# Half-size fetch, cast and transpose of one batch's tokens, earlier scores, and one shared transpose at the end: a change to a fused attention and feed-forward kernel

## The chip, the cores and the metric

The kernel runs on one core of a Trainium2 chip. The metric is the device time of one execution, in microseconds (us). Three timed runs of the kernel before gave 217.05, 218.31 and 218.33 us, median 218.31. A fourth, profiled execution took 216.83 us; all lines of the profile come from that one. Its span, from the first to the last instruction that the profiler recorded, is 214.6 us.

The engines: PE multiplies matrices (PEld is its loading of stationary weights), ACT (ScalarE) does activations and copies, DVE (VectorE) reductions, 32x32 transposes and elementwise work, POOL (GpSimd) copies and issues DMAs, SP (SyncE) only issues DMAs. Each engine runs its own instructions strictly in order.

## The reference

```
scores = scale * x @ state^T            # per batch and head: 512 tokens x 32 states, D = 64
a      = softmax over the 32 states;    xread = a @ state
a2     = softmax over the 512 tokens of scores^T;   sread = a2 @ x
rows   = concat(xread, sread) per batch, all 8 heads side by side (512 wide)
out    = leaky_relu(rows @ w_in) @ w_out          # 512 -> 2048 -> 512
```

There are 8 batches of 8 heads. The output has 8 x (512 + 32) rows of 512 fp32 numbers.

## The kernel before, in words

**Stages of one batch.** The tokens x of a batch (1 MB fp32) are fetched (`load_x`, L97), cast to bf16 in `xb` (`cast_x`, L104) and transposed to `xT`, from batch 2 on by a DMA that transposes (`a_xt_dma`, L188). `a_scores` (L201) multiplies `xT` with the batch's states into the PSUM tile `sc`, of which there is one. The states of batches 2 and 3 come through `load_state(0)` (L165, eight DMAs), a cast on POOL and a transposing DMA into `st_t` (`state_t`, L174). From `sc` two softmaxes start. Over the states: `a_shift` on DVE (maximum L215, its spreading L223, subtraction L225), `a_exp` on ACT (L232), `a_probs` on DVE (L237 to L247), which gives `aT`. Over the tokens: `a_max2` on DVE (L265), two `a_exp2` on ACT (L273), `a_probs2` on DVE (L286), then a transposing DMA (`a_a2t`, L291; batches 0 and 1 share one, L298) and `a_sread` (L305: 16 matmuls, two small ACT copies into `sr_t`).

**The feed-forward part.** `a_m` (L324) multiplies states with `w_in`, a quarter of its columns at a time, and `m_evict` (L344) copies the result to `M`. `ff1` (L354) then makes one of 16 slices of the hidden layer: two matmuls of `M` with `aT` into a PSUM tile `ph` (there are two), and a leaky ReLU on ACT (L362). `piece` (L379) does four of the 16 accumulating matmuls of one 128-row output tile `py` (L385); after the fourth piece the tile is copied by ACT or DVE (L394) and stored by SP (L400).

**Order.** It is written out by hand, engine by engine: each engine's instructions stand in the order of the calls. The main loop goes over batches b and, in each, over 16 steps s. A step is one `ff1` of b and, in batches 2 to 7 in every step, in batch 1 in every odd step, one `piece`. Everything else is hung on a step: in batch 1 (L673 to L698) the scores of batch 2 at step 4, its exponentials at steps 7, 9 and 11; in batch b from 2 on the scores of b+1 at step 1, the shared steps 5 to 7 for the exponentials, `a_sread` of b at step 8, and the transposes for it at step 0.

**Around the change.** Ahead of batch 1's loop (L638 to L667) stands batch 1's attention, mixed with batch 0's output pieces, and the preparation of batch 2: its `load_x` was issued long before on POOL's DMA queue, behind all weights (L539). At L648 comes the last eviction of batch 1's `M` on ACT, then its two `a_exp2` on ACT (L650), `state_t(0)` (L652), the cast of batch 2's heads 0 to 3 on ACT (L653) and 4 to 7 on POOL (L654), the transposing DMA of all of `xb` (L656), `a_probs(1)` on DVE, pieces of batch 0, and the stores with `load_x(3)` between them (L662 to L665).

Of the kernel before, what the change touches and what calls it, by code (L numbers as in the profile page):

```python
# [27 lines left out]
def kernel(  # L28
# [66 lines left out]
    xs, xl = {}, {}  # L95

    def load_x(b, eng):  # L97
        xl[b] = xpool.tile([P, H, NT * D], FP32, name="xl", tag="xl", bufs=2)
        eng.dma_start(xl[b][:], x[b].rearrange("h (p t) d -> p h (t d)", t=NT))

    def open_xb(b):
        xs[b] = xpool.tile([P, NT, H, D], BF16, name="xb", tag="xb")

    def cast_x(b, h0, h1, copy):  # L104
        copy(  # L105
            xs[b][:, :, h0:h1].rearrange("p t h d -> p h t d"),
            xl[b][:, h0:h1].rearrange("p h (t d) -> p h t d", t=NT),
        )

    def cast_x0(h0, h1, copy):  # L110
        u = h0 // NK
        copy(
            xs[0][:, :, h0:h1].rearrange("p t h d -> p h t d"),
            xf[u][:, h0 - NK * u:h1 - NK * u].rearrange("p h (t d) -> p h t d", t=NT),
        )

# [48 lines left out]
    def load_state(i):  # L165
        lo, hi = groups[i]
        for k in range(NK):
            for g in range(2):
# [2 lines left out]
                    state[lo:hi, 2 * k + g].rearrange("b n d -> n b d"),  # L171
                )

    def state_t(i):  # L174
        POO(stb[i][:], stf[i][:])
        nc.sync.dma_start_transpose(st_t[i][:], stb[i][:].rearrange("p b q -> p (b q)"))


# [4 lines left out]
    def a_open(a, b):  # L183
        a.b = b
        a.xb = xs[b]
        a.xT = att.tile([P, NT, NK, P], BF16, name="xT", tag="xT")

    def a_xt_dma(a):  # L188
        nc.sync.dma_start_transpose(
            a.xT[:].rearrange("p t k q -> p (t k) q"),  # L190
            a.xb[:].rearrange("p t h d -> p (t h d)"),
        )

    def st_of(a, g, k):
# [6 lines left out]
    def a_scores(a):  # L201
        sc = psum.tile([P, 2, S], FP32, name="sc", tag="sc", bufs=1)
        for k in range(NK):
            for g in range(2):
                nc.tensor.matmul(  # L205
                    sc[NS * k:NS * (k + 1), g, :],
                    lhsT=st_of(a, g, k),
                    rhs=a.xT[D * g:D * (g + 1), :, k, :],
                    start=True, stop=True,
                )  # L210
        a.sc = sc
# [7 lines left out]
        return m1  # L219

    def block_sub(flat, m1, n):
        m1b = att.tile([P, n, NS], FP32, name="mrowb", tag="mrowb")
        nc.vector.transpose(m1b[:], m1[:, :, None].to_broadcast([P, n, NS]))  # L223
        sh = att.tile([P, n * NS], FP32, name="sh", tag="sh")
        nc.vector.tensor_tensor(  # L225
            out=sh[:], in0=flat, in1=m1b[:].rearrange("p c j -> p (c j)"), op=ALU.subtract,
        )
        return sh
# [46 lines left out]
            bias=a.m2s[:, g:g + 1], scale=SCALE, accum_out=a.r2[:, g:g + 1],  # L275
        )

    a01 = consts.tile([P, 2, 2, S], BF16, name="a01")

    def a_probs2(a):  # L280
        nc.vector.tensor_scalar(out=a.r2[:], in0=a.r2[:], scalar1=1e-9, scalar2=None, op0=ALU.add)
        q2 = att.tile([P, 2], FP32, name="qc", tag="qc")
        nc.vector.reciprocal(q2[:], a.r2[:])
        a.a2 = a01[:, a.b] if a.b < 2 else att.tile([P, 2, S], BF16, name="a2", tag="a2", bufs=1)[:]
# [10 lines left out]
        )  # L295
        a.a2T = t[:]

    def a_a2t_01():  # L298
        t = consts.tile([P, 2, 2, NT, P], BF16, name="a01T")
        nc.sync.dma_start_transpose(  # L300
            t[:].rearrange("p b g i q -> p (b g i) q"), a01[:].rearrange("p b g s -> p (b g s)")
        )
        a0.a2T, a1.a2T = t[:, 0], t[:, 1]

    def a_sread(a):  # L305
        ps = psum.tile([P, NK, 2, NS], FP32, name="psr", tag="big", bufs=1)
        for k in range(NK):
            for i in range(NT):
                nc.tensor.matmul(  # L309
                    ps[:, k, :, :],  # L310
                    lhsT=a.xb[:, i, 2 * k:2 * k + 2, :].rearrange("p h d -> p (h d)"),
                    rhs=a.a2T[:, :, i, NS * k:NS * (k + 1)],
                    start=(i == 0), stop=(i == NT - 1),
                )
# [119 lines left out]
    def x0_half(u):  # L434
        pxt = [psum.tile([P, NT, P], BF16, name="pxth", tag=("ph", "py")[u]) for _ in range(2)]
        for v in range(2):
            for t in range(NT):
                h = NK * u + 2 * v
                nc.tensor.transpose(
                    pxt[v][:, t, :], a0.xb[:, t, h:h + 2, :].rearrange("p h d -> p (h d)"), ident[:]  # L440
                )
        return pxt

# [97 lines left out]
    open_xb(1)  # L541
    a_open(a1, 1)
# [71 lines left out]
            a_max2(a0)  # L614
    for u in range(2):
        VEC(
            a1.xb[:, :, NK * u:NK * (u + 1)].rearrange("p t h d -> p h t d"),
            x1[u][:].rearrange("p h (t d) -> p h t d", t=NT),
        )
    nc.vector.memset(stf[0][:, 0, D - 1:D + 1], 0.0)  # L620
# [7 lines left out]
    for u in range(2):  # L628
        ps = psum.tile([P, NT, 2, P], BF16, name="pxt2", tag="ph")
        for t in range(NT):  # L630
            for v in range(2):
                h = NK * u + 2 * v
                nc.tensor.transpose(
                    ps[:, t, v, :], a1.xb[:, t, h:h + 2, :].rearrange("p h d -> p (h d)"), ident[:]
                )
        VEC(a1.xT[:, :, 2 * u:2 * u + 2, :], ps[:])
        piece(0, h0, 2 + u, 0, bank=wide[:, u])
# [35 lines left out]
    for s in range(16):  # L673
        ff1(a1, h1, s)
        if s % 2:
            pb, hT, i, jq = fill[s // 2]
            piece(pb, hT, i, jq, copy=VEC if s == 3 else SCA)
        if s == 4:
            a_scores(a2)
            m_evict(a2, 0, a_m(a2, 0, "big"), SCA)  # L680
            a_shift(a2)
            a_max2(a2)
        elif s == 7:
            a_exp(a2)
            a_open(att_of[3], 3)
            a_xt_dma(att_of[3])
        elif s in (9, 11):
            a_exp2(a2, s // 2 - 4)
            if s == 9:
                a_probs(a2)  # L690
            else:
                a_probs2(a2)
        elif s == 13:
            a_probs2(a1)
            a_a2t_01()
# [7 lines left out]
    for b in range(2, B):  # L703
# [6 lines left out]
        for s in range(16):  # L710
            ff1(a, hT, s)
            if s == 0:
                if b + 2 < B:
                    load_x(b + 2, nc.sync)
                    open_xb(b + 2)
                a_a2t(a)
            elif s == 1:
                if nxt is not None:
                    a_scores(nxt)
                m_evict(a, 3, a_m(a, 3, "big"), SCA)  # L720
                if nxt is not None:
                    a_shift(nxt)
                    a_max2(nxt)
                if b + 2 < B:
                    cast_x(b + 2, 0, 8, POO)
            elif s == 4:
                if b == 2:
                    load_state(1)
                    a_sread(a0)
            elif s == 6:  # L730
                if b == 2:
                    a_sread(a1)
            elif s == 8:
                a_sread(a)
                if b == 2:
                    state_t(1)
            if nxt is not None:
                if s == 5:
# [67 lines left out]
```

## Time and profile before

| | |
|---|---|
| timed runs | 217.05, 218.31, 218.33 us (median 218.31) |
| profiled execution | 216.83 us, span 214.6 us |
| PE | busy 206.8 us, 96% of the span |
| ACT, DVE, POOL | 136.5 us (64%), 99.8 us (47%), 22.9 us (11%) |
| granted PE clock | 0.998 |
| DMA | 27.70 MB, mean 129 GB/s |

How to read it: "busy" is the time in which an engine had an instruction running. Matmuls are pipelined, and their recorded durations overlap, so the tight measure for PE is the distance between the starts of neighbouring matmuls; in dense stretches of the trace a 128x512 matmul follows the one before by 0.2155 us (four `piece` matmuls: 0.86). The few places where the distance is larger are what the kernel loses on PE. A line of the timeline gives start, duration, engine, line of the code, operation, tiles and count, and in brackets how long the engine had been idle before it and what ended that.

### The profile page before, as it was taken

The page shows a single profiled execution, that of the slowest core. Times are in us where ns is not written, and L with a number is a line of the kernel's source. Part 1 is how long each engine was busy: PE and PEld are TensorE (multiplying, and loading weights), DVE is VectorE, ACT ScalarE, POOL GpSimd, SP SyncE. Part 2 cuts the span into 40 slices and gives each one's busy share as a digit, 9 for nine tenths or more (in the row PEclk, how much of TensorE's full clock was granted, in tenths as well). Part 3 has the DMA queues.
Part 4 walks back from the last instruction along what each step waited for, and adds up shares of the span by engine and source line. Part 5 has one row for each costly group of instructions (what it writes and reads, how often), then busy time and mean ns, then how long its engine had stood idle before and what let it go on. Part 6 is the DMA issues. An engine that isn't in the chain of part 4 may idle for free.

```text
span 214.6 us, 3691 instructions
## 1 busy us (share of the span) xinstructions
PE 206.8 (96%) x1481; PEld 97.5 (45%) x1508; DVE 99.8 (47%) x153; ACT 136.5 (64%) x259; POOL 22.9 (11%) x37
## 2 busy tenths in 40 slices
PE   7899999999999999999999999999999999999993
PEld 2543434334454444444444444444444444466553
DVE  1678499699757236741784096706671000000000
ACT  3469576788788476856696579647784756464420
POOL 8840002030031030002100030000000000000000
PEclk9999999999999999999999999999999999999999
DMA  6999992975994981189216931452112111111123
GB/s 195 218 206 297 204 286 51 214 260 100 227 253 118 194 213 49 52 183 218 88 52 146 238 109 50 98 97 101 47 52 47 52 59 39 49 52 49 49 52 98
DMA packets 39856, 27.70 MB, mean 129 GB/s; under 512 B 24480, under 2 KB 35104, under 8 KB 39840
## 3 DMA queue, kind: packets, MB, share of 16 engines
q1 hardware_dynamic: 34912, 21.04, 38.8%
q0 software_dynamic: 4784, 6.29, 14.5%
q8 instruction: 12, 0.20, 0.4%
q10 hardware_dynamic: 144, 0.13, 0.3%
q14 instruction: 4, 0.03, 0.1%
HBM read 17.30 MB, written 8.91 MB: 122 GB/s over the span
## 4 chain that ended last, share of the span: by engine, by line
PE 77%; DMA 12%; DVE 6%; SPq 2%; issue 1%; POOL 1%; ACT 1%; POOLq 0%; ACTq 0%
PE py L385 44%; PE ph L357 19%; DMA x<-in_x_dram 7%; PE ph L368 3%; DMA stf<-in_state_dram 3%; PE pm L336 2%; DMA xT<-xb 2%; PE pspin L132 2%; PE psr L309 2%; PE pyh L411 2%; SPq L169 1%; PE sc L205 1%; DVE mrow L215 1%; DVE mrowb L223 1%; DVE qb L246 1%
## 5 line engine op out<-in xcount | busy, mean ns | idle before, releaser
L385 PE MATMUL py<-w_out_bf,hT 128*128 128x512 bf16 x442 | 116.1, 379 | 1.1
L362 ACT ACTIVATE hT<-ph 128x512 bf16<-128x512 f32 x112 | 66.6, 602 | 41.5 <-PE ph L357 41.5
L385 PEld LDWEIGHTS <-hT 128*128 128x128 bf16 x496 | 46.8, 98 | 56.9 <-issue 5.3
L357 PE MATMUL ph<-aT,M 128*128 128x512 bf16 x224 | 65.6, 379 | 0.4 <-ACT hT L362 0.4
L357 PEld LDWEIGHTS <-M 128*128 128x128 bf16 x224 | 21.7, 98 | 27.4 <-issue 1.7
L394 ACT COPY ysb<-py 128x512 f32<-128x512 f32 x30 | 17.6, 586 | 10.5 <-PE py L385 10.5
L215 DVE TRANSPOSE_TENSOR_REDUCE mrow<-sc 128x32 f32<-128x1024 f32 x7 | 8.8, 1250 | 31.6 <-PE sc L205 31.6
L416 DVE COPY ysh<-pyh 128x256 f32<-128x256 f32 x1 | 0.4, 425 | 47.7 <-PE pyh L411 47.7
L105 POOL CAST xb<-xl 128x2048 bf16<-128x2048 f32 (+1 forms) x6 | 10.5, 1753 | 77.1 <-DMA xl<-in_x_dram 42.7
L350 ACT CAST M<-pm 128x1024 bf16<-128x1024 f32 x13 | 13.2, 1013 | 1.7 <-PE pm L336 1.3
L237 DVE TRANSPOSE_TENSOR_REDUCE r<-e 128x32 f32<-128x1024 bf16 x7 | 8.7, 1243 | 10.1 <-ACT e L232 10.1
L350 DVE CAST M<-pm 128x1024 bf16<-128x1024 f32 x9 | 11.0, 1218 | 1.5 <-PE pm L336 1.5
L273 ACT ACTIVATE e<-sc,mcols 128x512 bf16<-128x512 f32 x16 | 11.2, 705 | 0.0
L348 DVE CAST M<-pm 128x512 bf16<-128x512 f32 x12 | 7.7, 685 | 6.1 <-PE pm L336 6.1
L265 DVE TENSOR_REDUCE mcol<-sc 128x2 f32<-128x1024 f32 x8 | 9.7, 1214 | 0.0
L372 ACT ACTIVATE hs<-ph 128x256 bf16<-128x256 f32 x16 | 6.0, 385 | 4.6 <-PE ph L368 4.4
L223 DVE STREAM_TRANSPOSE mrowb<-mrow 128x1024 f32<-128x1024 f32 x7 | 8.7, 1245 | 0.2
L246 DVE STREAM_TRANSPOSE qb<-qh 128x1024 bf16<-128x1024 bf16 x7 | 8.7, 1245 | 0.2
L225 DVE TENSOR_TENSOR sh<-sc,mrowb 128x1024 f32<-128x1024 f32 x7 | 8.6, 1224 | 0.2
L368 PE MATMUL ph<-sr_t,w_in_bf 128*128 128x256 bf16 x64 | 8.3, 273 | 0.0
L232 ACT ACTIVATE e<-sh 128x1024 bf16<-128x1024 f32 x7 | 7.3, 1050 | 1.1 <-DVE sh L225 1.1
L591 ACT ACTIVATE hT<-ph 128x512 bf16<-128x512 f32 x12 | 6.4, 597 | 2.1 <-PE ph L583 1.8
(97 smaller groups left out, 154.2 us busy)
## 6 DMA issues: line engine op xcount, KB each, us to landing
out_dram<-ysb SPq DMA_DIRECT2D x31, 256.0 KB, 2.3
xl<-in_x_dram SPq DMA_DIRECT2D x5, 1024.0 KB, 6.8
w_in_bf<-in_moe_w_in_dram POOLq DMA_DIRECT2D x4, 512.0 KB, 9.1
w_out_bf<-in_moe_w_out_dram POOLq DMA_DIRECT2D x4, 512.0 KB, 16.4
xf<-in_x_dram SPq DMA_DIRECT2D x2, 512.0 KB, 5.0
x<-in_x_dram POOLq DMA_DIRECT2D x2, 512.0 KB, 13.5
xl<-in_x_dram POOLq DMA_DIRECT2D x1, 1024.0 KB, 19.1
out_dram<-ysb SPq DMA_DIRECT2D x8, 64.0 KB, 1.7
```

The lines of the kernel that those rows point to most:

```text
L105: copy(xs[b][:, :, h0:h1].rearrange("p t h d -> p h t d"), xl[b][:, h0:h1].rearrange("p h (t d) -> p h t d", t=NT),)
L215: nc.vector.tensor_reduce(out=m1[:], in_=flat.rearrange("p (c j) -> p c j", j=NS), axis=AX.X, op=ALU.max, apply_transpose=True,)
L223: nc.vector.transpose(m1b[:], m1[:, :, None].to_broadcast([P, n, NS]))
L246: nc.vector.transpose(q1b[:], q1h[:, :, None].to_broadcast([P, n, NS]))
L265: nc.vector.tensor_reduce(out=m2[:], in_=a.sc[:], axis=AX.X, op=ALU.max, negate=True)
L273: nc.scalar.activation(out=a.e2[:, g], in_=a.sc[:, g, :], func=AF.Exp, bias=a.m2s[:, g:g + 1], scale=SCALE, accum_out=a.r2[:, g:g + 1],)
L350: copy(a.M[:, :, cols], pm[:])
L357: nc.tensor.matmul(ph[:], lhsT=a.M[:, g, P * j:P * (j + 1)], rhs=a.aT[:, g, :], start=(g == 0), stop=(g == 1),)
L362: nc.scalar.activation(out=hT[:, j, :], in_=ph[:], func=AF.Prelu, alpha=0.01)
L368: nc.tensor.matmul(ph[:, :n], lhsT=w_in_bf[:, k, P * j:P * (j + 1)], rhs=sr_t[:, k, :], start=(k == 0), stop=(k == NK - 1),)
L385: nc.tensor.matmul(y.py, lhsT=hT[:, j, P * i:P * (i + 1)], rhs=w_out_bf[:, j, :], start=(j == 0), stop=(j == 15),)
L394: copy(ysb[:], ys[b, i].py)
```

## The change

- Batch 2's tokens are fetched by two DMAs of four heads (512 KB) each, still from POOL's queue (`load_x_half`), where it was one of 1 MB. `xb` and `xT` of batch 2 are laid out as two halves, each contiguous.
- The casts of batch 2: heads 0 to 3 and then 4 and 5 on ACT, 6 and 7 on POOL. On ACT they stand ahead of batch 1's two `a_exp2`, where the one cast stood behind them.
- Two transposing DMAs, one for each half (`a_xt_half`), stand ahead of the state's on SP; the state's cast on POOL (`state_cast`) stays first there. `load_x(3)` follows at once, ahead of all four stores of batch 0 where one stood ahead of it.
- In batch 1's loop the scores of batch 2, with the first `a_m` and its eviction, come at step 3 (behind that step's piece) where they came at step 4 (behind that step's `ff1`). The output copy of step 3 goes to ACT instead of DVE.
- Batch 6's second probabilities are no longer transposed alone: both 6's and 7's lie in one tile and share a transposing DMA at step 0 of batch 7; `a_sread` of batch 6 moves from step 8 of batch 6 to step 6 of batch 7. The tiles of the pair 0/1 and of the pair 6/7 share memory.
- To make room or free it: `mrowb` has one buffer instead of two; batch 1's fetched tokens have tiles of their own instead of batch 0's.

```diff
+    def load_x_half(b, u):
+        if u == 0:
+            xl[b] = xpool.tile([P, H, NT * D], FP32, name="xl", tag="xl", bufs=2)
+        nc.gpsimd.dma_start(
+            xl[b][:, NK * u:NK * (u + 1)],
+            x[b, NK * u:NK * (u + 1)].rearrange("h (p t) d -> p h (t d)", t=NT),
+        )
...
+    def a_xt_half(a, u):
+        nc.sync.dma_start_transpose(
+            a.xTh[u].rearrange("p t k q -> p (t k) q"),
+            a.xb[u].rearrange("p t h d -> p (t h d)"),
+        )
...
-        m1b = att.tile([P, n, NS], FP32, name="mrowb", tag="mrowb")
+        m1b = att.tile([P, n, NS], FP32, name="mrowb", tag="mrowb", bufs=1)
...
-    x1 = [consts.tile([P, NK, 2 * P], FP32, name="x1", tag=f"xf{u}") for u in range(2)]
+    x1 = [consts.tile([P, NK, 2 * P], FP32, name="x1", tag=f"x1{u}") for u in range(2)]
...
-    load_x(2, nc.gpsimd)
+    for u in range(2):
+        load_x_half(2, u)
...
     m_evict(a1, 3, a_m(a1, 3, "ph"), SCA)
+    open_xb(2)
+    a_open(a2, 2)
+    cast_x(2, 0, 4, SCA)
+    state_cast(0)
+    cast_x(2, 4, 6, SCA)
+    cast_x(2, 6, 8, POO)
+    for u in range(2):
+        a_xt_half(a2, u)
+    state_t(0)
+    load_x(3, nc.sync)
+    open_xb(3)
     for g in range(2):
         a_exp2(a1, g)
-    open_xb(2)
-    state_t(0)
-    cast_x(2, 0, 4, SCA)
-    cast_x(2, 4, 8, POO)
-    a_open(a2, 2)
-    a_xt_dma(a2)
     a_probs(a1)
...
-    y_store(0, 2, VEC)
-    load_x(3, nc.sync)
-    open_xb(3)
-    y_store(0, 3, VEC)
-    cast_x(3, 0, 8, POO)
+    for i in (2, 3):
+        y_store(0, i, VEC)
+    cast_all(3)
...
-            piece(pb, hT, i, jq, copy=VEC if s == 3 else SCA)
-        if s == 4:
+            piece(pb, hT, i, jq)
+        if s == 3:
             a_scores(a2)
...
-                a_a2t(a)
+                if b == 7:
+                    a_a2t_pair(6)
+                elif b != 6:
+                    a_a2t(a)
...
             elif s == 6:
+                if b in (2, 7):
+                    a_sread(a1 if b == 2 else att_of[6])
+            elif s == 8:
+                if b != 6:
+                    a_sread(a)
                 if b == 2:
-                    a_sread(a1)
-            elif s == 8:
-                a_sread(a)
-                if b == 2:
+                    state_cast(1)
                     state_t(1)
```

PE has the same instructions in both kernels, in another order at two places.

More of the change, by code (lines that the diff above doesn't have):

```diff
@@ L99, in load_x, with pair_of, cast_all @@
         eng.dma_start(xl[b][:], x[b].rearrange("h (p t) d -> p h (t d)", t=NT))
-    def open_xb(b):
-        xs[b] = xpool.tile([P, NT, H, D], BF16, name="xb", tag="xb")
+    def load_x_half(b, u):
[5 more added lines that the diff above has]
+        )
+    def open_xb(b):
+        if b == 2:
+            t = xpool.tile([P, 2, NT, NK, D], BF16, name="xb", tag="xb")
+            xs[b] = [t[:, u] for u in range(2)]
+        else:
+            t = xpool.tile([P, NT, H, D], BF16, name="xb", tag="xb")
+            xs[b] = [t[:, :, NK * u:NK * (u + 1)] for u in range(2)]
+        xt[b] = t
+    def pair_of(a, t, k):
+        h = 2 * (k % 2)
+        return a.xb[k // 2][:, t, h:h + 2, :].rearrange("p h d -> p (h d)")
     def cast_x(b, h0, h1, copy):
+        u = h0 // NK
         copy(
-            xs[b][:, :, h0:h1].rearrange("p t h d -> p h t d"),
+            xs[b][u][:, :, h0 - NK * u:h1 - NK * u].rearrange("p t h d -> p h t d"),
             xl[b][:, h0:h1].rearrange("p h (t d) -> p h t d", t=NT),
+        )
+    def cast_all(b):
+        nc.gpsimd.tensor_copy(
+            xt[b][:].rearrange("p t h d -> p h t d"),
+            xl[b][:].rearrange("p h (t d) -> p h t d", t=NT),
         )
@@ L172, in load_state, with state_cast @@
                 )
+    def state_cast(i):
+        POO(stb[i][:], stf[i][:])
     def state_t(i):
-        POO(stb[i][:], stf[i][:])
         nc.sync.dma_start_transpose(st_t[i][:], stb[i][:].rearrange("p b q -> p (b q)"))
@@ L185, in a_open @@
         a.xb = xs[b]
-        a.xT = att.tile([P, NT, NK, P], BF16, name="xT", tag="xT")
+        if b == 2:
+            t = att.tile([P, 2, NT, 2, P], BF16, name="xT", tag="xT")
+            a.xTh = [t[:, u] for u in range(2)]
+        else:
+            t = att.tile([P, NT, NK, P], BF16, name="xT", tag="xT")
+            a.xTh = [t[:, :, 2 * u:2 * u + 2] for u in range(2)]
+        a.xT = t
     def a_xt_dma(a):
@@ L276, in a_exp2 @@
         )
-    a01 = consts.tile([P, 2, 2, S], BF16, name="a01")
+    pairs = {}
     def a_probs2(a):
@@ L283, in a_probs2 @@
         nc.vector.reciprocal(q2[:], a.r2[:])
-        a.a2 = a01[:, a.b] if a.b < 2 else att.tile([P, 2, S], BF16, name="a2", tag="a2", bufs=1)[:]
+        if a.b in (0, 6):
+            pairs[a.b] = att.tile([P, 2, 2, S], BF16, name="a2p", tag="a2p", bufs=1)
+        if a.b in (0, 1, 6, 7):
+            a.a2 = pairs[a.b - a.b % 2][:, a.b % 2]
+        else:
+            a.a2 = att.tile([P, 2, S], BF16, name="a2", tag="a2", bufs=1)[:]
         for g in range(2):
@@ L296, in a_a2t, with a_a2t_pair @@
         a.a2T = t[:]
-    def a_a2t_01():
-        t = consts.tile([P, 2, 2, NT, P], BF16, name="a01T")
+    def a_a2t_pair(b):
+        t = att.tile([P, 2, 2, NT, P], BF16, name="a2pT", tag="a2pT", bufs=1)
         nc.sync.dma_start_transpose(
-            t[:].rearrange("p b g i q -> p (b g i) q"), a01[:].rearrange("p b g s -> p (b g s)")
-        )
-        a0.a2T, a1.a2T = t[:, 0], t[:, 1]
+            t[:].rearrange("p b g i q -> p (b g i) q"),
+            pairs[b][:].rearrange("p b g s -> p (b g s)"),
+        )
+        for v in range(2):
+            att_of[b + v].a2T = t[:, v]
     def a_sread(a):
@@ L694 @@
             a_probs2(a1)
[L695 removed]
+            a_a2t_pair(0)
             pm = [a_m(a2, 1, "big"), a_m(a2, 2, "sc")]
```

19 lines of the change are left out of this document (10 added, 9 removed).

## The prediction

> **What bounds the kernel now.** I read the page's first table, then the starts of PE's matmuls in the timeline, then the chain that ended last for 24 to 60 us, then ACT and SP in the same stretch.
>
> ```profile
> PE 206.8 (96%) x1481; PEld 97.5 (45%) x1508; DVE 99.8 (47%) x153; ACT 136.5 (64%) x259; POOL 22.9 (11%) x37
> ```
>
> PE is the bound, so only holes between its matmuls can be won. From 36 us to the end the distances are 0.2155 us (0.31 where the tile size switches; a lone 0.43 is a record that is missing) except at two places:
>
> ```profile
> 38.70 1.03 PE L385 MATMUL py<-w_out_bf,hT 128*128 128x512 bf16 x4
> 39.56 0.59 PE L357 MATMUL ph<-aT,M 128*128 128x512 bf16 x2
> 40.60 0.41 PE L205 MATMUL sc<-xT,st_t 64*32 64x512 bf16 x8 [0.44 <-DMA xT<-xb]
> ...
> 45.07 1.03 PE L385 MATMUL py<-w_out_bf,hT 128*128 128x512 bf16 x4
> 46.49 1.08 PE L357 MATMUL ph<-aT,M 128*128 128x512 bf16 x4 [0.40 <-ACT hT L362]
> ```
>
> The scores of batch 2 could have started at 39.56 + 0.2155 + 0.31 = 40.09, so 0.51 us is lost at 40.60. The ff1 of step 10 could have started at 45.07 + 0.86 = 45.93: 0.56 lost, and 0.05 at step 11. The holes that the change can reach sum to 1.12 us. What made the first:
>
> ```profile
> 27.41 6.30 DMA stf<-in_state_dram
> ...
> 33.99 0.40 POOL stb L175
> 34.39 1.00 POOL xb L105
> ...
> 35.87 4.68 DMA xT<-xb
> 40.60 0.45 PE sc L205 x8
> 41.08 1.26 DVE mrow L215
> 42.36 1.26 DVE mrowb L223
> 43.64 1.23 DVE sh L225
> ```
>
> State and tokens land at 33.7 and 34.1, POOL casts both in turn, SP issues the state's transpose and only then the tokens', which lands at 40.55. The chain goes on through DVE to 44.86, and that makes the second hole:
>
> ```profile
> 43.09 1.08 ACT L362 ACTIVATE hT<-ph 128x512 bf16<-128x512 f32 x2 [0.23 <-PE ph L357]
> 44.90 1.06 ACT L232 ACTIVATE e<-sh 128x1024 bf16<-128x1024 f32 x1 [0.72 <-DVE sh L225]
> 45.86 1.07 ACT L362 ACTIVATE hT<-ph 128x512 bf16<-128x512 f32 x2
> ```
>
> ACT waits for `sh`, and the leaky ReLUs of steps 8 and 9 stand behind it; PE's step 10 needs a `ph` back.
>
> **The change, part by part.**
>
> *Fetch in halves.* The last `w_out` lands at 11.94 + 19.07 = 31.0, the tokens of batch 2 at 15.0 + 19.1 = 34.1, so half 0 should land near the middle, 32.6, half 1 at 34.1. Between is what the row of batch 1's tokens says, two DMAs of 512 KB issued at 8.31 and 9.06, landing after 12.7 and 14.4: 21.0 and 23.4, apart. The two together took 23.4 - 19.5 = 3.9 us behind the first `w_out` (7.58 + 11.9), the one of 1 MB 3.1: so half 1 lands between 34.1 and 34.9. I take 34.1, the row of the same tensor and moment. The issue of half 1 waits for the fourth `w_in` (5.21 + 11.7 = 16.9), but POOL's DMA queue has weights to move until 31.0: nothing.
>
> The Trainium skill, DMA: Bandwidth & Descriptors, "Rules for kernel authors", asks for 1 MiB or more per DMA, which speaks against this part; by the worse row, which agrees with it, half 1 at 34.9 makes the scores wait 0.1 us and the sum 0.65 instead of 0.75.
>
> *Casts.* ACT is free at 32.2. Heads 0 to 3: 32.6 + 1.05 (L105's row) = 33.7. Heads 4 and 5, a 128x512 cast of 0.62 (L112's row on ACT): 34.15 to 34.8. POOL: state 33.99 to 34.39 as before, then heads 6 and 7 in 0.52 (half of 1.04) to 0.79 (its L112 row): I take 0.6, to 35.0, as the low one is the same line's. Behind ACT's casts stand batch 1's two `a_exp2`, 1.47 us together (32.22 to 33.69), now until 36.25; ACT's next work is the leaky ReLU at 36.74, which had 1.55 us of idle time before it. So they are hidden, with 0.5 us left on ACT and about as much again before PE needs that `ph` back. `aT` of batch 1 on DVE (34.69, 1.23) can only gain from a shorter POOL cast, and PE is busy until 36.1 anyway.
>
> *Transposes.* No row shows a half. Bounds: 8 blocks as in the `a2T` rows, 1.27 to 2.66 us to issue and 3.0 to 6.8 to land; 16 blocks took 1.85 and 4.68, two blocks 1.27 and 2.4. The long rows stand behind a fetch of 1 MB (issue 54.28, then 2.56); the one at 159.66 with nothing in front took 1.30. Here nothing large is in front, so I take 1.27 and 3.0. SP: half 0 at 33.7 to 35.0, half 1 at 35.15 to 36.4, landing 38.2, state at 36.5 to 37.75, landing 38.9. Before it was 40.55.
>
> *SP behind them.* `load_x(3)` goes out at 37.8 instead of 38.90, the four stores of batch 0 behind it, the first 0.5 later than 37.82; nobody waits for them (`ysb` has four buffers). The cast and the transpose of batch 3 come about 1 us earlier and are wanted 0.8 earlier (scores at 54.20 without a wait): nothing.
>
> *Scores at step 3.* They stand behind the piece of 38.70, whose last matmul starts at 39.35: scores at 39.35 + 0.31 = 39.66, 0.76 behind the estimated landing. `sh` was ready 4.26 after the scores' start (40.60 to 44.86): now 43.92. DVE is free, since the copy that it had at 39.76 goes to ACT. On ACT this is new: copy 39.76 to 40.35, eviction of `M` (1.01) to 41.4, and only then the ReLUs of steps 4 and 5, ending 42.0 and 42.5. PE issues steps 4 and 5 at 40.22, the piece at 41.08, step 6 at 41.94: it waits 0.1 for the first `ph` and 0.07 for the second. Pieces and steps 8 and 9 follow to 45.55. ACT: exponential 43.95 to 45.0, ReLUs to 45.57 and 46.1. Step 10 starts at 45.60 (0.05 lost), step 11 loses 0.1, step 13 0.07. Left over: 0.35 to 0.4 of the 1.12.
>
> *Batches 6 and 7.* One transpose of 8 blocks goes, one grows to 16 (the row of batches 0 and 1: 1.83 to issue, 4.9 to land). It goes out at 159.66, as the one of batch 7 did; batch 6's `a_sread`, two steps (2.6 us) ahead of the one at 178.19, comes at 175.6, some 11 us after the landing. Its 16 matmuls (0.47) and two ACT copies (0.54) move from one dense batch to the next: nothing. `mrowb` is written and read by DVE alone in order, the own tiles of batch 1 replace no wait that the timeline shows (POOL issues at 7.58, 8.31, 9.06 back to back): nothing.
>
> *Sum.* 1.12 - 0.37 = 0.75 us. Against the profiled execution: 216.83 - 0.75 = 216.1. That execution is 1.5 below the median 218.31; the four runs shown lie in two pairs, mean 217.63, and I have no reason to expect one pair: 217.63 - 0.75 = 216.9.
>
> **The rivals.**
>
> *The halves land together.* Then ACT does both casts from 34.15 to 35.8, the `a_exp2` end at 37.3, the ReLUs of batch 1's first steps are 0.56 late (PE loses about 0.2), the last transpose lands at 40.25 and the scores start at 40.3: gain 0.25, time 217.4. Against it: batch 1's halves landed 2.4 us apart. The Trainium skill, DMA: Bandwidth & Descriptors, "Two DMAs through the same engine are not ordered", says that nothing orders transfers across the 16 DMA engines, so this could be; the row just named speaks for order here.
>
> *Slower: the half transposes cost what the `a2T` rows mostly do.* With 2.54 us to issue each, SP is done with the halves at 38.85, the state's transpose lands at 41.3, scores at 41.35. Since everything behind the scores now stands on one step less of slack, no gain is left when they start at 40.5, and each microsecond beyond costs one: +0.85, time 218.5. For it: the median landing of those rows is 6.6. Against: the fetch in front of them.
>
> *All of the holes go.* If ACT's copy and eviction collide less than worked out, 1.1 us: 216.5.
>
> **How the numbers follow.** Forecast 0.55, halves together 0.12, all holes 0.10, slow transposes 0.15, something that I do not see 0.08, either way. A measurement of this kernel tells about 1% from no change: 216.13 or less, 220.49 or more. My likeliest moves the four runs to 216.1, 216.3, 217.55 and 217.6, so only a median out of the fast pair, or more gain, comes under 216.13: 0.20. Slower by 1% needs 2.2 us, more than any case prices: 0.07. The range goes from the fastest run with all holes gone, 215.7, to the slow rival, 218.6.
>
> **What would show it.** In the profile after: half 0 of `xl` landing over 1 us before half 1; SP's three transposes within 33.7 to 38; scores at about 39.7 with no DMA wait; the step 10 ff1 at 45.6 and the span 213.8. Waits of ACT on the tokens beyond 35, transposes of over 2 us to issue, or a new PE hole at step 6 of over 0.2 would make it wrong; so would any change of PE's distances after 55 us.

## The result and the profile after

| | before | after |
|---|---|---|
| timed runs | 217.05 to 218.65 us, median 218.33 (7 runs) | 216.52 to 217.07 us, median 216.80 (7 runs) |
| ratio after / before | | 0.9934, 95% interval 0.9913 to 0.9956 |
| profiled execution, span | 216.83, 214.6 us | 216.83, 214.4 us |
| PE busy | 206.8 us | 207.1 us |

The changed kernel is 1.53 us faster by the medians, and its runs lie closer together. The forecast was 216.9 us. The two profiled executions take the same 216.83 us, so a comparison of these two profiles alone would show no gain at all: the one of before was 1.5 us below the median of its kernel, the one of after was close to the median of its own.

The first table of the page of after:

```profile
PE 207.1 (97%) x1482; PEld 97.4 (45%) x1508; DVE 99.4 (46%) x152; ACT 137.8 (64%) x261; POOL 23.2 (11%) x38
```

PE is still the bound. PE in the timeline of after, from the first step of batch 1 (36.56) on:

```profile
36.56 1.03 PE L405 MATMUL ph<-aT,M 128*128 128x512 bf16 x4
...
39.15 1.03 PE L433 MATMUL py<-w_out_bf,hT 128*128 128x512 bf16 x4
40.15 0.41 PE L246 MATMUL sc<-xT,st_t 64*32 64x512 bf16 x8
...
45.12 1.03 PE L433 MATMUL py<-w_out_bf,hT 128*128 128x512 bf16 x4
46.05 1.08 PE L405 MATMUL ph<-aT,M 128*128 128x512 bf16 x4
46.97 1.02 PE L433 MATMUL py<-w_out_bf,hT 128*128 128x512 bf16 x4
48.08 1.08 PE L405 MATMUL ph<-aT,M 128*128 128x512 bf16 x4
```

The scores follow their piece after 1.00 us, where a distance without a hole is 0.96 (three times 0.2155 and 0.31): the hole of 0.51 is down to 0.04. Step 10 follows after 0.93 instead of 1.42: 0.07 is left of 0.56. But step 12, at 48.08, follows its piece after 1.11, so there is a hole of 0.25 at a place where the profile shown of before had none.

SP, in the same timeline: the two half transposes together, the state's, and the fetch of batch 3.

```profile
34.16 2.72 SPq L230 DMA_TRANSPOSE xT<-xb  x2
36.94 1.24 SPq L205 DMA_TRANSPOSE st_t<-stb  x1
38.23 0.57 SPq L99 DMA_DIRECT2D xl<-in_x_dram  x1
```

The trace has them landing at 37.51, 39.79 and 40.11. ACT, again in the timeline of after:

```profile
33.09 1.04 ACT L126 CAST xb<-xl 128x1024 bf16<-128x1024 f32 x1 [0.31 <-DMA xl<-in_x_dram]
34.48 0.62 ACT L126 CAST xb<-xl 128x512 bf16<-128x512 f32 x1 [0.34 <-DMA xl<-in_x_dram]
...
36.25 0.20 ACT L314 ACTIVATION_READ_ACCUMULATOR e<-sc,mcols 128x1 f32 x1
37.19 1.09 ACT L410 ACTIVATE hT<-ph 128x512 bf16<-128x512 f32 x2 [0.74 <-PE ph L405]
...
44.45 1.06 ACT L273 ACTIVATE e<-sh 128x1024 bf16<-128x1024 f32 x1 [0.27 <-DVE sh L266]
45.42 1.07 ACT L410 ACTIVATE hT<-ph 128x512 bf16<-128x512 f32 x2
46.76 0.69 ACT L314 ACTIVATE e<-sc,mcols 128x512 bf16<-128x512 f32 x1 [0.28 <-DVE mcols L308]
```

The two halves of the tokens are cast as they land (33.07 and 34.46), batch 1's `a_exp2` behind them end at 36.45, and ACT is then idle for 0.74 until PE has a `ph` ready. The wait for `sh` that made the second hole of before has shrunk from 0.72 to 0.27. New is the last line: the exponential `a_exp2` of batch 2 waits for `mcols`, and the leaky ReLUs that PE needs at step 12 stand behind it. What `mcols` waits for is seen on DVE and POOL, in the same timeline:

```profile
44.34 1.21 DVE L306 TENSOR_REDUCE mcol<-sc 128x2 f32<-128x1024 f32 x1
45.59 1.08 DVE L308 TENSOR_SCALAR mcols<-mcol 128x2 f32<-128x2 f32 x1
...
44.75 1.90 POOL L132 CAST xb<-xl 128x2048 bf16<-128x2048 f32 x1 [9.62 <-DMA xl<-in_x_dram]
```

`mcols` scales two numbers per partition. It takes 0.17 us in the profile shown of before and 1.08 here, and it ends at 46.67, when POOL's cast of batch 3's tokens ends (46.65). The reduction ahead of it, 1.21 us beside the same cast, is not held up.

### The profile page after: what moved, and what is told of

It is laid out like the page before. It is cut to its first block, busy times and chain, and to the rows that moved or that the text cites. A ratio compares the mean times of both kernels' runs of the same rounds, so it can differ in the third digit from the quotient of the medians.

```text
span 214.4 us, 3689 instructions
## 1 busy us (share of the span) xinstructions
PE 207.1 (97%) x1482; PEld 97.4 (45%) x1508; DVE 99.4 (46%) x152; ACT 137.8 (64%) x261; POOL 23.2 (11%) x38
## 4 chain that ended last, share of the span: by engine, by line
PE 87%; DMA 5%; DVE 3%; POOL 2%; issue 1%; ACT 1%; POOLq 0%; ACTq 0%
PE py L433 48%; PE ph L405 21%; DMA w_in_bf<-in_moe_w_in_dram 5%; PE pm L384 4%; PE ph L416 3%; PE pyw L433 3%; PE ph L632 2%; PE psr L357 2%; PE pyh L459 2%; PE sc L246 1%; POOL w_in_bf L145 1%; DVE mrow L256 1%; DVE mrowb L264 1%; DVE M L398 1%; DVE sh L266 1%
## 5 line engine op out<-in xcount | busy, mean ns | idle before, releaser
L442 ACT COPY ysb<-py 128x512 f32<-128x512 f32 x31 | 18.2, 586 | 10.7 <-PE py L433 10.7
L256 DVE TRANSPOSE_TENSOR_REDUCE mrow<-sc 128x32 f32<-128x1024 f32 x7 | 8.7, 1250 | 32.6 <-PE sc L246 32.6
L132 POOL CAST xb<-xl 128x2048 bf16<-128x2048 f32 x5 | 9.5, 1894 | 77.4 <-DMA xl<-in_x_dram 44.7
```

The lines of the kernel that those rows point to most:

```text
L132: nc.gpsimd.tensor_copy(xt[b][:].rearrange("p t h d -> p h t d"), xl[b][:].rearrange("p h (t d) -> p h t d", t=NT),)
L256: nc.vector.tensor_reduce(out=m1[:], in_=flat.rearrange("p (c j) -> p c j", j=NS), axis=AX.X, op=ALU.max, apply_transpose=True,)
L442: copy(ysb[:], ys[b, i].py)
```

## The experiments

Two theories stand for the 1.53 us. The forecast's: the change closes the two holes of the profile shown, 0.6 to 0.75 us, and the rest is chance between runs. Theory P: in most executions of before there is a third hole, at step 12, because POOL's cast of batch 3's tokens holds `mcols`, and the change closes most of that one too. Beside these stands the question which part of the change earns the time. Every kernel below was timed in five rounds against before on the same chip; "before" in the table is the median of before in the same group of runs. There were three groups on three chips (e1 to e4; e6 to e9; e5 and e10 to e12), and only the last one holds after again (e11). So where a kernel of the first two groups is set against after's 216.80 us, tenths are uncertain, and the ratios to before are the better measure.

| kernel | median (lowest to highest), us | before | ratio and 95% interval |
|---|---|---|---|
| e1: before, unchanged | 218.01 (217.14 to 218.38) | 218.25 | 0.9996 (0.9978 to 1.0014) |
| e2: before + shared transpose of 6 and 7 | 218.04 (217.26 to 218.41) | 218.25 | 0.9994 (0.9976 to 1.0013) |
| e3: after without the shared transpose | 217.18 (217.00 to 218.36) | 218.25 | 0.9966 (0.9950 to 0.9982) |
| e4: after with scores at step 4 | 216.98 (216.31 to 217.24) | 218.25 | 0.9947 (0.9931 to 0.9964) |
| e5: before + scores at step 3 | 217.60 (216.98 to 218.49) | 218.19 | 0.9985 (0.9968 to 1.0002) |
| e6: after, tokens in one fetch | 217.66 (216.62 to 218.22) | 218.04 | 0.9978 (0.9959 to 0.9997) |
| e7: before + batch 3's cast in pieces | 217.45 (216.73 to 217.66) | 218.04 | 0.9970 (0.9957 to 0.9984) |
| e8: after + batch 3's cast in pieces | 216.49 (216.39 to 216.54) | 218.04 | 0.9936 (0.9918 to 0.9954) |
| e9: after, one transpose behind the state's | 217.31 (216.41 to 218.13) | 218.04 | 0.9967 (0.9950 to 0.9985) |
| e10: e8 without the shared transpose | 216.79 (216.71 to 217.03) | 218.19 | 0.9944 (0.9925 to 0.9962) |
| e11: after, unchanged | 216.76 (216.65 to 216.98) | 218.19 | 0.9942 (0.9925 to 0.9959) |
| e12: e8 again | 216.64 (216.41 to 216.73) | 218.19 | 0.9934 (0.9916 to 0.9951) |

Where a profile is compared, it goes by three starts on PE, which divide the execution into parts that the change can and cannot reach: the first step of batch 1, the scores of batch 3 (18 steps later), and the last matmul.

| profile of | step 0 of batch 1 | scores of batch 3 | between | last matmul | profiled time |
|---|---|---|---|---|---|
| before, the one shown | 36.11 | 54.20 | 18.09 | 211.04 | 216.83 |
| e1 (before again) | 36.72 | 55.52 | 18.80 | 212.36 | 218.13 |
| e5 (scores at step 3) | 36.73 | 54.85 | 18.12 | 211.69 | 217.48 |
| after | 36.56 | 54.07 | 17.51 | 210.90 | 216.83 |
| e11 (after again) | 36.51 | 54.36 | 17.85 | 211.20 | 216.98 |
| e6 (one fetch) | 36.63 | 55.67 | 19.04 | 212.51 | 218.14 |
| e9 (one transpose) | 36.76 | 54.77 | 18.01 | 211.61 | 217.47 |
| e8 (cast in pieces) | 36.61 | 53.77 | 17.16 | 210.60 | 216.39 |
| e12 (cast in pieces) | 36.81 | 53.97 | 17.16 | 210.81 | 216.73 |

From the scores of batch 3 to the last matmul every one takes 156.83 or 156.84 us: nothing behind 55 us has changed on PE.

**e1, before a second time.** Nothing is edited; the question is whether the first profile shows the usual execution.

> The kernel before, unchanged, for more profiled and timed executions of it. Six of its seven timed runs lay at 218.1 to 218.65 us, while its profiled execution took 216.83 and the changed kernel's seven runs 216.5 to 217.1. Theory A (slack): in the usual execution batch 2's tokens or its state land later than in the profiled one, and each 0.1 us of that delays the scores of step 4; the spans of this kernel then differ by some 1.4 us, and a profile that takes about 218.3 shows a wait of 1.5 to 2 us ahead of the scores. Rival B: the usual executions lose 1.4 us at another place that the first profile does not show (batches 3 to 7, the tail, the start). Rival C: the profiled execution is simply as usual and the runs are longer for reasons of the chip; then the two kernels do not keep their distance here.

Its profiled execution took 218.13 us, 1.30 more than the first. Of these, 0.61 is already there at step 0 of batch 1 (36.72 against 36.11); PE's first product of `a_m`, 0.56 later (11.44 against 10.88), shows that it comes from the first 11 us. The other 0.71 is between. PE, POOL, DVE and ACT in the timeline of e1:

```profile
40.17 0.59 PE L357 MATMUL ph<-aT,M 128*128 128x512 bf16 x2
41.15 0.41 PE L205 MATMUL sc<-xT,st_t 64*32 64x512 bf16 x8 [0.38 <-DMA xT<-xb]
...
47.05 1.08 PE L357 MATMUL ph<-aT,M 128*128 128x512 bf16 x4 [0.40 <-ACT hT L362]
47.96 1.02 PE L385 MATMUL py<-w_out_bf,hT 128*128 128x512 bf16 x4
49.53 1.08 PE L357 MATMUL ph<-aT,M 128*128 128x512 bf16 x4 [0.54 <-ACT hT L362]
...
46.20 1.90 POOL L105 CAST xb<-xl 128x2048 bf16<-128x2048 f32 x1 [10.26 <-DMA xl<-in_x_dram]
46.58 1.54 DVE L267 TENSOR_SCALAR mcols<-mcol 128x2 f32<-128x2 f32 x1
48.22 0.69 ACT L273 ACTIVATE e<-sc,mcols 128x512 bf16<-128x512 f32 x1 [0.73 <-DVE mcols L267]
48.90 1.07 ACT L362 ACTIVATE hT<-ph 128x512 bf16<-128x512 f32 x2
```

Read from the bottom: the ReLUs of steps 10 and 11 start at 48.90, behind an exponential that waited 0.73 for `mcols`; `mcols` ends at 48.12, the cast at 48.10; step 12 follows its piece after 1.57 us, where 0.86 is dense. That is a third hole of 0.70 us, beside 0.45 at the scores and 0.56 at step 10. In the profile shown of before `mcols` came first by 0.12 us, and the third hole did not appear. DVE and POOL in the timeline of before:

```profile
46.03 0.17 DVE L267 TENSOR_SCALAR mcols<-mcol 128x2 f32<-128x2 f32 x1
...
46.15 1.90 POOL L105 CAST xb<-xl 128x2048 bf16<-128x2048 f32 x1 [10.78 <-DMA xl<-in_x_dram]
...
47.38 0.70 DVE L241 TENSOR_SCALAR r<-r 128x32 f32<-128x32 f32 x1
```

The last line shows that the hold could have been seen in the profile on which the forecast rests. Another small scaling on DVE (L241) started while the same cast ran. It took 0.70 us, where it takes 0.18 at 32.80, and ended at 48.08, just behind the cast (48.05). It cost PE nothing there.

**e2, the shared transpose of batches 6 and 7 alone, on the kernel before.**

```diff
-        a.a2 = a01[:, a.b] if a.b < 2 else att.tile([P, 2, S], BF16, name="a2", tag="a2", bufs=1)[:]
+        if a.b in (0, 6):
+            pairs[a.b] = att.tile([P, 2, 2, S], BF16, name="a2p", tag="a2p", bufs=1)
+        if a.b in (0, 1, 6, 7):
+            a.a2 = pairs[a.b - a.b % 2][:, a.b % 2]
...
-                a_a2t(a)
+                if b == 7:
+                    a_a2t_pair(6)
+                elif b != 6:
+                    a_a2t(a)
...
-                if b == 2:
-                    a_sread(a1)
+                if b in (2, 7):
+                    a_sread(a1 if b == 2 else att_of[6])
```

> The kernel before with the shared transpose of batches 6 and 7 alone. Theory A: no change, 218.3 us within 0.2, the same spread as before. Rival B (the usual loss lies in the last batches, or in how the tiles lie in memory): about 1.4 us faster, 216.8.

218.04 us, a ratio of 0.9994 (0.9976 to 1.0013): nothing, on this base. Its profile shows the third hole's cause once more on before's order: POOL's cast at 45.58, `mcols` at 46.57 held for 0.93, to 47.50, with the cast's end at 47.47. But that hold is short enough to leave only 0.11 us at step 12 (47.94 to 48.91), so of the two profiles of before's order in which the cast holds `mcols`, one has a large third hole.

**e3, everything but the shared transpose.**

```diff
-                if b == 7:
-                    a_a2t_pair(6)
-                elif b != 6:
-                    a_a2t(a)
+                a_a2t(a)
...
-                if b in (2, 7):
-                    a_sread(a1 if b == 2 else att_of[6])
+                if b == 2:
+                    a_sread(a1)
...
-                if b != 6:
-                    a_sread(a)
+                a_sread(a)
```

> The changed kernel with batches 6 and 7 transposed each alone again. Theory A: 216.8 us within 0.2, all of the gain. Rival B: the gain, or most of it, is gone, 218.3.

217.18 us, 0.4 above after, though the shared transpose alone gained nothing in e2. The profile puts the difference behind the last matmul: from its start to the end of the profiled time, e3 takes 217.28 - 211.06 = 6.22 us, the profile of after 5.93, e11 5.78 and before 5.79. (Ahead of it e3's step 0 is 0.43 later than after's and its stretch between 0.28 shorter; `mcols` took only 0.85 us.) The trace shows what happens at the end. SP closes its program with a row of waits, one for each of the semaphores on which its DMAs report in turn, and each takes some 0.06 us even if nothing is left to wait for. In after SP issues 79 DMAs, the last store reports on the semaphore that is waited for last, and SP is through 0.08 us after the landing (213.50 to 213.58). In e3 it issues 80, the last store reports on one that stands early in the row, and seven more waits follow: 0.51 us (213.67 to 214.18). e10 below also has 80 DMAs and the same 0.51; all other runs have 78 or 79 and 0.08 to 0.14. So the 0.43 us are not a gain of transposing two batches together: the pair takes away the one DMA that the halves had added on SP.

**e4, the scores back at step 4.**

```diff
-            piece(pb, hT, i, jq)
-        if s == 3:
+            piece(pb, hT, i, jq, copy=VEC if s == 3 else SCA)
+        if s == 4:
             a_scores(a2)
```

> The changed kernel with the scores of batch 2, their first product with w_in and DVE's output copy at step 4 again; halves, order of the transposes and the pair stay. Theory A: what counts is how early the last transpose lands; PE reaches the scores 0.43 us later, the chain over DVE and ACT starts 0.43 later and the leaky ReLU of step 4 is no longer behind the eviction: 0.1 to 0.4 us slower than the changed kernel, 216.9 to 217.2, and well below 218.3. Rival: the earlier place of the scores is the gain, 217.8 to 218.3.

216.98 us, 0.18 above after, but the intervals of the two ratios overlap, so a difference is not shown. PE in the timeline of e4:

```profile
40.40 0.41 PE L246 MATMUL sc<-xT,st_t 64*32 64x512 bf16 x8
...
44.88 1.03 PE L433 MATMUL py<-w_out_bf,hT 128*128 128x512 bf16 x4
46.30 1.08 PE L405 MATMUL ph<-aT,M 128*128 128x512 bf16 x4 [0.39 <-ACT hT L410]
```

Half a step later there is no wait for the transposes at all, but the hole of 0.56 at step 10 is back (44.88 to 46.30 is 1.42). The place of the scores trades one for the other; in this execution step 0 started at 36.42, and with the hole it arrives at batch 3 after 17.76.

**e5, the scores at step 3 alone, on the kernel before.** The same edit the other way round, with before's whole fetch, cast and transpose.

> The kernel before with the scores of batch 2, their first product with w_in and the output copy on ACT at step 3; fetch, casts and transposes as before. The transpose lands at 40.5 to 41 either way, so the scores start no earlier and wait 0.43 us more; ACT has the copy and the eviction ahead of the leaky ReLUs of steps 4 and 5: no gain, 218.0 to 218.4 where the kernel before has 218.2 (interval on both sides of 1). Rival: the earlier place itself is worth something, 217.5 or less.

217.60 us, ratio 0.9985 (0.9968 to 1.0002): a little below what was expected, and not told from none. Its profile has one hole where before has two: the scores stand at 41.24, 0.96 late, and step 10 is dense.

```profile
39.32 1.03 PE L385 MATMUL py<-w_out_bf,hT 128*128 128x512 bf16 x4
41.24 0.41 PE L205 MATMUL sc<-xT,st_t 64*32 64x512 bf16 x8 [0.90 <-DMA xT<-xb]
```

That sum is close to e1's (0.96 against 0.45 + 0.56), so without earlier tokens the earlier place is not seen to be worth anything. The profile alone would not settle it: 15 of the 16 DMA engines were done with the transpose at 39.95, ahead of the 40.28 at which PE could have taken up the scores, and the last one at 41.20. That its profiled time is 0.65 below e1's is the third hole, absent here because POOL's cast came late, at 48.07, when `mcols` (46.67) was long done.

**e6, the tokens of batch 2 in one fetch, the rest as after.**

```diff
-    for u in range(2):
-        load_x_half(2, u)
+    load_x(2, nc.gpsimd)
```

> The changed kernel with batch 2's tokens fetched by one DMA of 1 MB; casts, transposes in halves and everything else as changed. If the fetch in halves matters: ACT can start its first cast only at about 34.2 us instead of 33.1, both casts end about 1 us later, the last transpose lands near 41 and batch 1's leaky ReLUs start late: 0.4 to 1 us slower than the changed kernel, 217.2 to 217.8. If the casts and transposes are limited elsewhere (the second half lands at the same time either way): within 0.2 us of it, 216.8.

217.66 us: 0.86 above after, where the forecast's rival "the halves land together" priced it at 0.5 (217.4 against 216.9). ACT and PE in the timeline of e6:

```profile
34.61 1.57 ACT L126 CAST xb<-xl 128x1024 bf16<-128x1024 f32 x2 [1.75 <-DMA xl<-in_x_dram]
...
39.22 1.03 PE L433 MATMUL py<-w_out_bf,hT 128*128 128x512 bf16 x4
41.16 0.41 PE L246 MATMUL sc<-xT,st_t 64*32 64x512 bf16 x8 [0.91 <-DMA st_t<-stb]
...
47.97 1.02 PE L433 MATMUL py<-w_out_bf,hT 128*128 128x512 bf16 x4
49.69 1.08 PE L405 MATMUL ph<-aT,M 128*128 128x512 bf16 x4 [0.69 <-ACT hT L410]
```

ACT waits for the tokens until 34.61 instead of 33.09, so the scores are 0.98 late; and as their whole chain then meets POOL's cast (`mcols` held for 1.68), the third hole is 0.86 us. Five of its twelve runs lie at 216.6 to 217.0, which is where after lies, and seven at 217.6 to 218.2; the profile is one of the seven, and what the five do was not seen. So the 0.86 is the difference of the medians and not what one fetch costs in every execution.

**e9, the state's transpose first and one whole transpose behind it, the rest as after.** The tiles `xb` and `xT` of batch 2 are laid out whole again for it, too.

```diff
-    for u in range(2):
-        a_xt_half(a2, u)
     state_t(0)
+    a_xt_dma(a2)
```

> The changed kernel with the state's transpose first on SP and then one transposing DMA of all of batch 2's tokens; fetch and casts in halves stay. The two halves took 3.35 and 4.18 us to land in the profile and the state's, last in the row, landed at 40.11. If the transposes in halves are what brings the scores forward: the whole one, issued at about 35.2, lands 4.7 later at 39.9 plus up to 0.7 for the transfers behind it, the scores wait 0.3 or more and the time rises to 217.1 to 217.5. If the casts alone do it: it lands at 39.8 to 40.0, no wait, 216.8 within 0.2.

217.31 us, 0.5 above after; here too the runs lie in two groups, four at 216.4 to 216.7 and eight at 217.2 to 218.1. SP and PE in the timeline of e9:

```profile
34.31 1.27 SPq L205 DMA_TRANSPOSE st_t<-stb  x1
35.77 1.92 SPq L224 DMA_TRANSPOSE xT<-xb  x1
...
39.35 1.03 PE L433 MATMUL py<-w_out_bf,hT 128*128 128x512 bf16 x4
41.17 0.41 PE L246 MATMUL sc<-xT,st_t 64*32 64x512 bf16 x8 [0.79 <-DMA xT<-xb]
```

The whole transpose starts when the last head is cast, 1.6 us later than the first half in after, and lands at 41.13: the scores are 0.86 late. But by the trace 15 of the 16 DMA engines were done with it at 40.27, and PE could have taken up the scores at 40.31; the wait is that of the last engine, which took 0.86 longer. So this profile doesn't show that a whole transpose is too slow as such, and four of the runs are as fast as after. What the halves of the transpose are worth by themselves stays open.

**e7 and e8, batch 3's cast in four pieces of two heads,** on before and on after. If theory P holds, `mcols` gets in between two pieces.

```diff
-    cast_x(3, 0, 8, POO)
+    for h in range(0, 8, 2):
+        cast_x(3, h, h + 2, POO)
```

> The kernel before with POOL's cast of batch 3 cut into four of two heads. In three profiles a small DVE operation (the scaling of the maxima, 0.17 us elsewhere) took 0.93, 1.54 and 1.08 us and ended together with POOL's cast of 1.9 us. Theory P (port): DVE's operation is held until POOL's instruction ends, and that is the third hole of PE, 0.7 us at step 12, in the usual execution of the kernel before. Then with pieces of 0.5 to 0.6 us the operation ends by about 47.0, the hole at step 12 shrinks under 0.2, and the time falls from 218.2 to 217.4 to 217.7, with less spread. Rival: the coincidence of the ends means nothing, or DVE does not get in between pieces that follow each other: 218.2, hole unchanged.

> The changed kernel with the same cut of batch 3's cast. Theory P: its rest of a hole at step 12, 0.25 us in the profile, goes: 216.4 to 216.7, 0.1 to 0.4 us faster than the changed kernel. Rival: no change, 216.8, or slower if DVE is held once for each piece.

On before the median falls by 0.59 us, ratio 0.9970 (0.9957 to 0.9984), as theory P expects, and no run is above 217.66, where 21 of before's own 29 runs beside it are, up to 218.47. Its profile can't show how, since the fetch of batch 3 came late in it (cast at 47.84, `mcols` at 46.63 in 0.17 us). On after it is seen; DVE, POOL and PE in the timeline of e8:

```profile
45.59 0.42 DVE L308 TENSOR_SCALAR mcols<-mcol 128x2 f32<-128x2 f32 x1
...
44.82 2.29 POOL L126 CAST xb<-xl 128x512 bf16<-128x512 f32 x4 [9.87 <-DMA xl<-in_x_dram]
...
46.97 1.02 PE L433 MATMUL py<-w_out_bf,hT 128*128 128x512 bf16 x4
47.83 1.03 PE L405 MATMUL ph<-aT,M 128*128 128x512 bf16 x4
```

The cast runs over the same time as in after (44.82 against 44.75), `mcols` starts at the same 45.59, and it now ends at 46.01, close to the end of the second piece (44.82 + 2 x 0.57 = 45.96) instead of that of the whole. Step 12 follows after 0.86: the third hole is gone. Beside it only some hundredths change on PE: the scores stand 0.04 sooner, and the piece behind step 12 0.05.

All fourteen profiles together say the same. `mcols` starts 5.43 or 5.44 us after the scores in every one; what differs is how long it takes, and the hole at step 12 follows that:

| profile | e6 | e1 | e11 | after | e4 | e2 | e3 | e12, e8, e9 | before, e5, e7, e10 |
|---|---|---|---|---|---|---|---|---|---|
| `mcols` takes, us | 1.68 | 1.54 | 1.38 | 1.08 | 0.95 | 0.93 | 0.85 | 0.65, 0.42, 0.36 | 0.17 |
| hole at step 12, us | 0.86 | 0.70 | 0.54 | 0.25 | 0.13 | 0.11 | 0.02 | 0 | 0 |

The hole is what `mcols` takes beyond about 0.83 us; a shorter hold is covered by slack, and costs nothing.

**e10, e11, e12: the cast in pieces without the shared transpose, after, and the cast in pieces again,** on one chip. e11 and e12 edit nothing that was not shown; e10 has the edits of e3 and e8 together.

> The changed kernel with batch 3's cast cut in four and with batches 6 and 7 transposed each alone. Cut alone it took 216.4 to 216.55, so a small effect of the pair can be told here. If the pair is hidden, as forecast: 216.5 within 0.15. Rival (the changed kernel without the pair took 217.18, the changed kernel 216.8): the pair is worth 0.3 us, 216.8 or more.

> The changed kernel, unchanged, beside the two with the cut cast on the same chip: 216.8 within 0.2.

> The changed kernel with batch 3's cast cut in four, again, beside the changed kernel on the same chip: 216.5, 0.3 us below it, if theory P (DVE's small operation is held by POOL's long cast) explains the rest of the hole at step 12; if the first result was a matter of the chip, both take the same time.

216.79, 216.76 and 216.64 us. e11 has `mcols` held for 1.38 us (to 46.97; the cast ends at 46.95) and a hole of 0.54 at step 12; e12 has 0.65 and no hole. Between the scores that is 17.85 against 17.16, yet the times differ by 0.12 in the median and 0.25 in the profiled executions: e12 began step 0 by 0.30 later and took 0.14 more behind the last matmul. Whether the later step 0 is chance is open (it lies at 36.11 in the profile shown of before and between 36.4 and 37.0 in the thirteen others). So the cast in pieces is clearly faster than before, but against after it gains 0.12 us on the one chip that had both, about as much as these runs can tell; the 0.31 between e8 and after is across chips, and their ratios to before (0.9936 and 0.9934) don't show it. e10 ends like e3: 216.97 - 210.71 = 6.26 us behind the last matmul, 0.34 more than e12, with the same seven waits of SP behind the last landing.

## Why the prediction was right, and which step of it failed

The time, 216.80 against 216.9, was right. The mechanism of the two holes that the forecast saw was right too, but the base was 0.70 us too low and the gain 0.78 too small. These two nearly cancel, so that the time came out to 0.1 us is luck. By its steps:

*The two holes and what is left of them.* Right. Everything on PE in the profile of after is 0.45 later, because step 0 is. Less that, the scores stand at 39.70 (forecast 39.66) and step 10 at 45.60 (forecast 45.60). Against the profile shown of before, the gain between is 18.09 - 17.51 = 0.58, where 0.75 was forecast. The third hole of 0.25 takes the rest, and the forecast's own 0.07 for step 13 was not lost.

*Fetch in halves.* Right in kind: 33.07 and 34.46, 1.39 apart (forecast 32.6 and 34.1). By the medians it is the largest single part that was tried, 0.86 us (e6), though e6 is as fast as after in five of its twelve runs. The Trainium skill, DMA: Bandwidth & Descriptors, "Rules for kernel authors", asks for 1 MiB or more per DMA where bandwidth is the goal; here the measurement decides for the two of 512 KB, as the first half is worked on while the second one still flows, and the second one lands no later than the one fetch of e6 (34.46 against 34.59).

*Casts and `a_exp2` ahead of the first step.* Right: 36.45 against the forecast's 36.25, and ACT still idles for 0.74 behind them.

*Transposes.* The issue was right (1.34 and 1.27 against 1.27), the landing too short: 3.35, 4.18 and 3.17 us after their issue, where the forecast's times make it 3.0, 3.0 and 2.4. The state's, the last, is 0.76 later than forecast beyond the shift of the whole execution, and the slack was 0.76. So the scores waited 0.04 us, and a slightly slower transpose would have shown at once: e9's transpose lands 1.02 later than after's last and its scores start 1.02 later. The rival "the half transposes cost what the `a2T` rows mostly do" was off in its issue of 2.54, but the direction of its worry was right.

*"The cast and the transpose of batch 3 come about 1 us earlier and are wanted 0.8 earlier (scores at 54.20 without a wait): nothing."* This step failed. It asked whether PE needs the transpose earlier and not what else the cast touches while it runs. POOL's cast holds `mcols` on DVE until it ends, and the exponential and the ReLUs behind it wait. The forecast had a like effect in hand for `aT`, which "can only gain from a shorter POOL cast" (1.23 us before, 0.69 in after), and didn't ask the question for `mcols`. In after the cast comes 1.45 us earlier than in e1 and `mcols` 1.0, and the hold falls from 1.37 to 0.91 us (less its own 0.17) and the hole from 0.70 to 0.25.

*"The four runs shown lie in two pairs, mean 217.63, and I have no reason to expect one pair."* This failed with it. The profiled 216.83 was the exception, below every timed run of before: e1 and the first profile differ by 0.61 up to step 0 and by 0.71 behind it, nearly all of it the third hole. Against an execution like e1 (218.13, near before's medians of 218.0 to 218.3), after gains 0.45 - 0.04 at the scores, 0.56 - 0.07 at step 10 and 0.70 - 0.25 at step 12, together 1.35, less some hundredths at the new neighbours: 1.29 by the table of starts, of 1.53 by the medians. The remainder is within what step 0's start varies by. How often each of the two chances falls on an execution of before was not counted: of the five profiles in which the cast comes in before's order (e5 and e7 among them), only e1 has a large third hole. That it is usual is argued from the timed runs, whose upper part is missing in e7.

*Scores at step 3.* Right that ACT carries it without a new PE hole at steps 4 to 6; its worth, 0.18 us in e4, is not told from none, and none is shown without the halves (e5).

*Batches 6 and 7: nothing.* Right on the path that was costed (e2). Beside the halves the pair is worth 0.15 to 0.4 us by the medians (e10 and e3), through SP's closing waits, which the forecast did not look at.

The rival "all of the holes go", 1.1 us, is near the gain that came, but not by its mechanism: what it missed was a hole that its profile did not show.

## What to carry to other kernels

Before a sum is made against one profiled execution, ask where its time lies among the timed runs. If it lies at their edge, look for small instructions that started just ahead of or behind a long one on a neighbouring engine, or that took several times what they take elsewhere: an order that was decided by 0.12 us in the first profile was decided the other way in the next two (e1 and e2). Cutting the first transfer of a chain in two can pay where work can start on the first half and everything behind it waits, even against a rule for large DMAs. A slack worked out for a chain of DMA transposes should allow for landings later than the fastest rows say (0.35, 1.18 and 0.77 us here). And a change that adds or takes away a DMA can move the closing waits at the end of the program, far from the place of the change.

## What the runs showed of the hardware that was not expected

A DVE instruction of 0.17 us was held for as long as a POOL instruction ran, and no longer. End of `mcols` and end of POOL's cast: 48.12 and 48.10 (e1), 47.50 and 47.47 (e2), 46.67 and 46.65 (after), 46.97 and 46.95 (e11), 48.27 and 48.25 (e6); the same holds for L241 in the profile shown of before (48.08 and 48.05). With the cast in four pieces it ended near the end of the second piece (e8). A maximum over 1024 columns on DVE (1.21 us) ran beside the same cast without delay, and `mcols` that started 0.12 us ahead of the cast took 0.17. The Trainium skill, SBUF — State Buffer, "Who interferes with whom", says that DVE and GpSimd share a pair of ports, that a `tensor_scalar` can use it where its operands allow and a `tensor_reduce` never does on this chip, and that whichever comes first keeps it for the whole instruction while the other fully blocks. The trace agrees where POOL comes first: the held instruction is a `tensor_scalar`, the free one a `tensor_reduce`, and the hold ends with the instruction of POOL. That POOL is held where DVE comes first is not shown by these runs.

The whole transposing DMA of e9 landed on 15 of 16 DMA engines at 40.27 and on the last at 41.13, so a single engine set the time that PE waited for. The same transpose shows it in e5 (39.95 and 41.20) and e7 (39.98 and 41.16), and the state's in e3 (39.31 and 40.06) and e12 (39.14 and 39.86). In the other transposing DMAs of the fourteen profiles the last engine is less than 0.3 us behind the rest; why one engine is late was not tried.
